# Reading LayerNorm rows back from DRAM as two transfers instead of one

## The chip, the cores and the metric

The kernel runs on one core of a Trainium2 chip. A core has a matrix engine (PE, with its weight loads shown as PEld), a vector engine (DVE), an activation engine (ACT), a general engine (POOL) and a queue engine (SP) that issues most of the DMA transfers; each works through its own list of instructions in order and waits on counters that the others raise. The metric is the device time of one execution in microseconds (us). A profile shows one execution; times inside it are counted from the start of its span.

## The reference

Two layers of sliding-window attention and two of a dense MLP follow each other, with the same weights both times. Input is one sequence of 2048 tokens of 512 channels in bf16; there are 32 heads of 16 channels, a window of 256 tokens and 1792 hidden channels.

```python
def _A_ref(x, wqkv, wo):
    H = 32; Dh = D // H; W = 256
    qkv = (x @ wqkv).reshape(B, S, 3, H, Dh).transpose(2, 0, 3, 1, 4)
    q, k, v = qkv[0], qkv[1], qkv[2]
    scores = jnp.einsum("bhqd,bhkd->bhqk", q, k) * (Dh ** -0.5)
    mask = (idx[:, None] - idx[None, :] >= 0) & (idx[:, None] - idx[None, :] < W)
    p = _softmax(jnp.where(mask[None, None], scores, -1e9), axis=-1)
    return jnp.einsum("bhqk,bhkd->bhqd", p, v).transpose(0, 2, 1, 3).reshape(B, S, D) @ wo

def _B_ref(x, w1, b1, w2, b2):
    return _gelu(x @ w1 + b1) @ w2 + b2

x = x + _A_ref(_layernorm(x), A_wqkv, A_wo)
x = x + _B_ref(_layernorm(x), B_w1, B_b1, B_w2, B_b2)
x = x + _A_ref(_layernorm(x), A_wqkv, A_wo)
x = x + _B_ref(_layernorm(x), B_w1, B_b1, B_w2, B_b2)
```

## The kernel before

The tokens are cut into 16 tiles of 128 rows. Counted over the two rounds there are 32 tiles (`tau`), and each passes two LayerNorms: one ahead of the attention (layer 0) and one ahead of the MLP (layer 1). The residual stream `X` and all weights stay in on-chip memory (SBUF).

Attention works in blocks of two tiles. For a block, PE makes queries, keys and values from the normalised, transposed rows `xnTA`; it then makes scores in visits of 512 columns (`ps<-QT,KT` in the profile), ACT takes their exponentials (line 946, `E<-ps`), DVE or POOL multiply the mask (line 967), PE multiplies by the values (`ps<-E,Va`), DVE transposes and normalises the result, and PE projects it with `Wo`. The MLP runs in jobs of two or four tiles: PE multiplies the rows `xnTB` by `W1` (shown as `ps<-xnTB,W_sb`), ACT applies the gelu (lines 1104 and 1112), PE multiplies by `W2` (`ps<-W_sb,gT`), and DVE adds the residual (line 788). The work of MLP jobs is laid in between the visits of later attention blocks, so that PE has something to do while ACT takes exponentials.

The matrix products need the normalised rows with channels on the partitions, that is transposed. `layernorm` (from line 726) makes mean and variance on DVE (lines 732 and 734), the reciprocal root on POOL (line 739) and the scaled rows `xn` on DVE (line 742). Then there are two ways. For the first tiles and the last two, PE transposes through PSUM. For the others (`by_dma`), DVE transposes blocks of 32 x 32 into `xs_` (line 751), SP writes `xs_` to one of eight scratch buffers in DRAM (line 756), and SP reads the scratch back into `xnTA` or `xnTB` in another layout (line 758). The write has 128 rows of 1 KB. The read fills, on each of the 128 partitions, four row groups (`r` in the code) of 256 bytes; in DRAM the four groups lie one after the other, so each group is a contiguous quarter of the scratch buffer. The 44 tiles that take this way give 44 writes and 44 reads, 26 into `xnTB` and 18 into `xnTA`.

The order in which the work is issued is written out by hand: `ORDER` lists all 3239 operations, `TURNS` picks the engine where there is a choice, and `BANKS` gives the PSUM banks. `_List.run` walks that list and computes a planned start and end of each operation from its planned duration `dur` and, for a transfer, the time `issue` after which SP is taken to be free; the plan does not change the order. `_Sched.op` then turns dependences into waits. Each transfer gets one of 16 counters in turn, and raises it by 16 once it has landed; whoever needs the data waits for the counter's value. `spread` may move a PE wait to an earlier matmul if the plan says that it will be over by then.

Both transfers of a tile go through SP's queue in order, with the other tiles' transfers and the output's (lines 1127 and 1141). A read first waits on SP until its write has landed, and while SP waits, everything listed behind it waits too.

Of the kernel before, what the change touches and what calls it, by code (L numbers as in the profile page):

```python
# [55 lines left out]
class _Sched:  # L56
# [29 lines left out]
                    kn[c2] = v2  # L86
        return True

    def op(self, eng, fn, reads=(), writes=(), inc=1, dma=False, start=0.0, end=0.0, n=1, joins=(), behind=None):
        kn = self.know[eng]  # L90
        req = {}

        def need(c, v):
            if v > 0 and kn.get(c, 0) < v and req.get(c, 0) < v:
                req[c] = v

        counter = eng
        if dma:
            counter = "dma%d" % (self.dma_rr % self.N_DMA_SEMS)
            self.dma_rr += 1  # L100
            inc = 16
            need(counter, self.cnt_val[counter])
        held = [self.res_w[r] for r in reads if r in self.res_w]
        for w in writes:
            if w in self.res_w:
                held.append(self.res_w[w])
            held += self.res_r.get(w, {}).items()
        for c, v in held:
            if not c == eng == "pe":
                need(c, v)  # L110
        for r in joins:
            need(*self.res_w[r])
        if behind is not None:
            need(*behind)
        waits = sorted(req.items(), key=lambda x: -self.when[x])
        waits = [(c, v) for c, v in waits if self._acquire(eng, c, v)]
        val = self.cnt_val[counter] + inc
        self.cnt_val[counter] = val
        self.snap[(counter, val)] = dict(kn)
        self.when[(counter, val)] = end  # L120
        for r in reads:
            d = self.res_r.setdefault(r, {})
            if d.get(counter, 0) < val:
                d[counter] = val
        for wr in writes:
            self.res_w[wr] = (counter, val)
            self.res_r[wr] = {}
        self.prog[eng].append(dict(fn=fn, waits=waits, counter=counter, inc=inc, start=start, n=n))
        return counter, val

    def wait_all_dma(self, eng):
# [32 lines left out]
    def emit(self):  # L164
        nc = self.nc
        self.spread()
        with nc.Block() as block:
            for eng in self.ENGINES:
                prog = self.prog[eng]

                def run(e, _prog=prog, _pe=eng == "pe"):
                    for o in _prog:
                        if _pe:
                            r = o["fn"](_Slots(e, o["at"]))
                        else:
                            for c, v in o["waits"]:
                                e.wait_ge(self.cnt_sem[c], v)
                            if o["fn"] is None:
                                continue
                            r = o["fn"](e)  # L180
                        r.then_inc(self.cnt_sem[o["counter"]], o["inc"])

                block._start_engine(run, _ENG_TYPES[eng])


class _List:
# [11 lines left out]
        self.lr = {}  # L198

    def add(self, eng, fn, dur, reads=(), writes=(), prio=0.0, alloc=(), free=(), after=(), geo=None, table=None,  # L200
            issue=0.0, alt=(), war=(), lock=False, joins=()):

        i = len(self.nodes)
        deps = set(after)
        for r in tuple(reads) + tuple(joins):
            if r in self.lw:
                deps.add(self.lw[r])
        for w in tuple(writes) + tuple(war):
            if w in self.lw:
                deps.add(self.lw[w])  # L210
            deps.update(self.lr.get(w, ()))
        for r in reads:
            self.lr.setdefault(r, []).append(i)
        for w in writes:
            self.lw[w] = i
            self.lr[w] = []
        deps.discard(i)
        n = 0
        if eng == "pe":
            c = _Count()  # L220
            fn(c, _Anywhere())
            n = c.n
        self.nodes.append(dict(
            eng=eng, fn=fn, dur=dur, reads=list(reads), writes=list(writes), prio=prio, joins=tuple(joins),
            jdeps=frozenset(self.lw[r] for r in joins), alloc=alloc, free=tuple(free), deps=deps, geo=geo, table=table,
            issue=issue, lock=lock, alts=((eng, fn, dur),) + tuple(alt), n=n, behind=None,
            heavy=any(a[0] == "pool" and a[2] > 600.0 for a in ((eng, fn, dur),) + tuple(alt)),
        ))
        return i
# [69 lines left out]
def bass_interleave_layers__sliding_block__dense_activation_gelu__prompt_kernel(  # L299
# [13 lines left out]
    P = 128  # L313
# [61 lines left out]
    with ExitStack() as kctx:  # L375
# [255 lines left out]
        add = PL.add  # L631
# [45 lines left out]
        for n, took in ((8, 3560.0), (3, 1280.0)):  # L677
            add("pe", clear(n), took, reads=["zero", "g0"], writes=["ps:init0", "ps:init1"], prio=-200, geo="f")

        def dma(fn, writes, reads=(), dur=2200.0, prio=0.0, issue=640.0, eng="sp"):  # L680
            add(eng, fn, dur, reads=reads, writes=writes, prio=prio, issue=issue)

        queued = {"sp": 0, "act": 0}

# [40 lines left out]
        def layernorm(tau, layer, dst, dname, prio):  # L725

            t = tau % T
            k = 2 * tau + layer
            s = xn_rr[0] % NXN
            xn_rr[0] += 1  # L730
            k6 = xn_rr[0] % 8
            add("dve", lambda e, B: e.bn_stats(stat6[:, k6, :], X[:, t, :]), 590,  # L732
                reads=["X%d" % t], writes=["st%d" % k6], prio=prio)
            add("dve", lambda e, B: e.bn_aggr(statmv[:, k, :], stat6[:, k6, :]), 95,
                reads=["st%d" % k6], writes=["mv%d" % k], prio=prio - 300)
            eps = lambda e, B: e.tensor_scalar(  # L736
                out=statmv[:, k, 1:2], in0=statmv[:, k, 1:2], scalar1=EPS, scalar2=None, op0=ALU.add)
            add("dve", eps, 75, reads=["mv%d" % k], writes=["ve%d" % k], prio=prio - 300, alt=(("pool", eps, 130),))
            add("pool", lambda e, B: e.tensor_tensor(  # L739
                out=statmv[:, k, 1:2], in0=statmv[:, k, 1:2], in1=mhalf[:], op=ALU.pow), 535,  # L740
                reads=["ve%d" % k, "mhalf"], writes=["rs%d" % k], prio=prio - 500)
            scale = lambda e, B: e.tensor_scalar(
                out=xn[:, s, :], in0=X[:, t, :], scalar1=statmv[:, k, 0:1], scalar2=statmv[:, k, 1:2],
                op0=ALU.subtract, op1=ALU.mult)
            add("dve", scale, 325, reads=["X%d" % t, "mv%d" % k, "rs%d" % k], writes=["xn%d" % s], prio=prio, lock=True)
            g = "tp%d" % k
            if by_dma(tau, layer):
                z = xs_rr[0] % NXS
                v = xs_rr[0] % NSC
                xs_rr[0] += 1  # L750
                add("dve", lambda e, B: e.transpose(  # L751
                    xs_[:, z, :].rearrange("p (q d j) -> p d q j", q=4, d=DC), xn[:, s, :].rearrange("p (d j q) -> p d q j", q=4, d=DC)), 630,
                    reads=["xn%d" % s], writes=["xs%d" % z], prio=prio)
                flat = scr[v].rearrange("p c -> (p c)")
                room = 0.0 if tau < 12 else 700.0
                dma(lambda e, B: e.dma_start(scr[v], xs_[:, z, :]),
                    ["scr%d_0" % v], reads=["xs%d" % z], prio=prio, dur=2200.0 + room, issue=400.0)
                dma(lambda e, B: e.dma_start(dst.rearrange("p r d j -> p r (d j)"), flat.rearrange("(r p c) -> p r c", r=4, p=P)),
                    [dname], reads=["scr%d_0" % v], prio=prio, dur=2700.0 + 2 * room, issue=400.0)
                return  # L760
            def tr(e, B):
                for c in range(DC):
                    r = e.transpose(psb[:, B[g][0], c * P : (c + 1) * P], xn[:, s, c * P : (c + 1) * P], ident[:])
                return r

            add("pe", tr, 4 * 56.0, reads=["xn%d" % s, "ident"], writes=["ps:" + g], prio=prio,
                alloc=[(g, 1)], geo="f", war=[dname])
            evac(lambda B: dst.rearrange("p r c j -> p c r j"),
                 lambda B: psb[:, B[g][0], 0 : DC * P].rearrange("p (c r j) -> p c r j", c=DC, r=4), 512,
                 ["ps:" + g], [dname], prio, free=[g], two=True, kind="t", boot=True)  # L770
# [386 lines left out]
        B = PL.gmap  # L1157
# [13 lines left out]
        for i in order:  # L1171
            nd = PL.nodes[i]
            n = 1
            if nd["eng"] == "pe":
# [1 line left out]
                nd["fn"](c, B)  # L1176
                n = c.n
            marks[i] = S_.op(nd["eng"], lambda e, fn=nd["fn"]: fn(e, B), reads=phys(nd["reads"]), writes=phys(nd["writes"]), dma=nd["issue"] > 0,
                  start=nd["start"], end=nd["vis"], n=n, joins=nd["joins"], behind=marks[nd["behind"]])
        S_.wait_all_dma("sp")  # L1180
        S_.emit()

# [27 lines left out]
```

## Time and profile before

| | us |
|---|---|
| median of 3 runs | 448.62 (447.82 to 449.89) |
| profiled execution | 448.7 |
| its span in the profile | 446.6 |
| PE busy in the span | 432.3 |
| ACT busy | 388.2 |
| DVE busy | 376.2 |
| POOL busy | 250.2 |

In the profile's rows, `L758` is line 758 of the kernel, an engine's name with a `q` at its end (`SPq`) is its sequencer issuing something, and `xnTB<-scr_x` is an operation that writes `xnTB` from `scr_x`. In rows of a timeline stand the start, the length, the engine, the line, the operation, the number of merged instructions (`x3`) and, in brackets, the idle time before it with what ended that. A row with three numbers and slashes gives the shortest, the median and the longest, in nanoseconds for durations. "DMA to landing" is the time from the start of the issue until the data has landed. A span's share of busy time does not say what is critical; the chain of work that ended last does, since it is followed back from the last instruction through whatever released each step.

### The profile page before, as it was taken

The page shows a single profiled execution, that of the slowest core. Times are in us where ns is not written, and L with a number is a line of the kernel's source. Part 1 is how long each engine was busy: PE and PEld are TensorE (multiplying, and loading weights), DVE is VectorE, ACT ScalarE, POOL GpSimd, SP SyncE. Part 2 cuts the span into 40 slices and gives each one's busy share as a digit, 9 for nine tenths or more (in the row PEclk, how much of TensorE's full clock was granted, in tenths as well). Part 3 has the DMA queues.
Part 4 walks back from the last instruction along what each step waited for, and adds up shares of the span by engine and source line. Part 5 has one row for each costly group of instructions (what it writes and reads, how often), then busy time and mean ns, then how long its engine had stood idle before and what let it go on. Part 6 is the DMA issues. An engine that isn't in the chain of part 4 may idle for free.

```text
span 446.6 us, 19315 instructions
## 1 busy us (share of the span) xinstructions
PE 432.3 (97%) x8762; PEld 230.7 (52%) x8762; DVE 376.2 (84%) x744; ACT 388.2 (87%) x457; POOL 250.2 (56%) x311
## 2 busy tenths in 40 slices
PE   7989999988999999999999999999999999999997
PEld 4545645645544555454445445445454454445664
DVE  6999989999997999889998999999898886687602
ACT  3999999999999989898998999889988998892442
POOL 5665875756888355363845682643448655562510
PEclk9999999999999999999999999999999999999999
DMA  9920000001120132001320002300222003102012
GB/s 260 370 94 4 4 1 4 4 15 26 46 66 13 27 86 63 25 10 32 95 51 3 26 25 65 83 4 13 73 62 62 15 3 84 28 3 86 13 35 70
DMA packets 39902, 22.87 MB, mean 51 GB/s; under 512 B 24588, under 2 KB 39308, under 8 KB 39820
## 3 DMA queue, kind: packets, MB, share of 16 engines
q1 hardware_dynamic: 39404, 21.24, 16.5%
q8 instruction: 68, 1.11, 1.0%
q10 hardware_dynamic: 416, 0.39, 0.3%
q14 instruction: 14, 0.11, 0.1%
HBM read 13.77 MB, written 7.86 MB: 48 GB/s over the span
## 4 chain that ended last, share of the span: by engine, by line
PE 70%; ACT 21%; DVE 4%; DMA 3%; issue 1%; POOL 1%
PE ps L32 70%; ACT E L946 13%; ACT gT L1104 3%; ACT gT L1112 2%; ACT L946 1%; DMA scr_x<-xs_ 1%; DMA xnTB<-scr_x 1%; ACT L1104 1%; DVE stat L732 1%; DMA X<-in_A_x_dram 1%; PE ps L36 1%; DVE TT L1032 1%; DVE E L967 0%; DVE X L788 0%; DVE xs_ L751 0%
## 5 line engine op out<-in xcount | busy, mean ns | idle before, releaser
L946 ACT ACTIVATE E<-ps 128x1024 bf16<-128x1024 f32 x304 | 286.2, 1054 | 19.8 <-PE ps L32 18.8
L967 POOL TENSOR_TENSOR E<-E,mask 128x512 bf16<-128x512 bf16 (+1 forms) x142 | 147.2, 1055 | 81.5 <-DVE E L967 31.4
L32 PE MATMUL ps<-W_sb,gT 128*128 128x512 bf16 (+2 forms) x462 | 118.9, 374 | 0.5 <-ACT E L946 0.5
L32 PE MATMUL ps<-xnTB,W_sb 128*128 128x512 bf16 (+1 forms) x560 | 114.1, 337 | 1.1 <-DMA xnTB<-scr_x 1.0
L32 PEld LDWEIGHTS ps<-xnTB,W_sb 128*128 128x128 bf16 x560 | 51.3, 98 | 45.5 <-ACT E L946 3.3
L32 PE MATMUL ps<-xnTA,Wqkv_sb 128*128 128x256 bf16 (+1 forms) x544 | 73.3, 267 | 1.0 <-ACT E L946 0.7
L32 PE MATMUL ps<-QT,KT 32*64 32x320 bf16 (+4 forms) x2976 | 65.3, 258 | 2.7 <-ACT E L946 1.6
L788 DVE TENSOR_TENSOR X<-X,ps 128x512 bf16<-128x512 bf16 x63 | 42.4, 677 | 24.5 <-PE ps L32 23.2
L32 PEld LDWEIGHTS ps<-W_sb,gT 128*128 128x128 bf16 x462 | 40.2, 98 | 42.7 <-issue 6.4
L32 PEld LDWEIGHTS ps<-xnTA,Wqkv_sb 128*128 128x128 bf16 x544 | 46.8, 98 | 22.3 <-issue 3.7
L1112 ACT ACTIVATE gT<-ps,b1T 128x512 bf16<-128x512 f32 (+1 forms) x68 | 36.4, 584 | 23.5 <-PE ps L32 23.4
L1076 POOL TENSOR_TENSOR X<-X,b2b 128x512 bf16<-128x512 bf16 x32 | 36.7, 1155 | 31.7 <-DVE E L967 20.0
L32 PEld LDWEIGHTS ps<-QT,KT 32*64 32x64 bf16 x2976 | 27.8, 103 | 49.5 <-ACT E L946 33.4
L1101 DVE TENSOR_SCALAR gT<-ps,b1T 128x512 bf16<-128x512 f32 (+1 forms) x72 | 45.2, 650 | 9.0 <-PE ps L32 8.3
L967 DVE TENSOR_TENSOR E<-E,mask 128x512 bf16<-128x512 bf16 (+1 forms) x120 | 46.2, 412 | 3.9 <-ACT E L946 3.7
L1032 DVE STREAM_TRANSPOSE TT<-ps 128x1024 f32<-128x1024 f32 x32 | 39.8, 1245 | 10.0 <-PE ps L32 9.7
L32 PE MATMUL ps<-E,Va 64*17 64x128 bf16 (+3 forms) x3872 | 46.1, 229 | 2.3 <-ACT E L946 1.2
L32 PEld LDWEIGHTS ps<-E,Va 64*17 64x17 bf16 x3872 | 36.8, 85 | 18.9 <-PE ps L32 7.3
L732 DVE BATCH_NORM_STATS2 stat<-X 128x6 f32<-128x512 bf16 x64 | 43.1, 681 | 2.3 <-DMA X<-in_A_x_dram 2.0
L739 POOL TENSOR_TENSOR statmv<-statmv,mhalf 128x1 f32<-128x1 f32 x64 | 37.1, 586 | 10.9 <-DVE statmv L736 7.6
L862 DVE TENSOR_TENSOR KT<-ps,parmask 128x1024 bf16<-128x1024 f32 x30 | 36.2, 1207 | 1.5 <-PE ps L32 0.9
L32 PE MATMUL ps<-Wo_sb,OT 128*128 128x512 bf16 x128 | 36.3, 380 | 0.2 <-ACT E L946 0.2
(55 smaller groups left out, 343.4 us busy)
## 6 DMA issues: line engine op xcount, KB each, us to landing
scr_x<-xs_ SPq DMA_DIRECT2D x44, 128.0 KB, 2.0
W_sb<-in_B_w_dram SPq DMA_DIRECT2D x2, 1792.0 KB, 15.6
xnTB<-scr_x SPq DMA_DIRECT2D x26, 128.0 KB, 2.7
xnTA<-scr_x SPq DMA_DIRECT2D x18, 128.0 KB, 2.6
out_dram<-X SPq DMA_DIRECT2D x15, 128.0 KB, 1.8
Wqkv_sb<-in_A_wqkv_dram SPq DMA_DIRECT2D x4, 256.0 KB, 4.9
X<-in_A_x_dram SPq DMA_DIRECT2D x1, 1024.0 KB, 9.1
Wqkv_sb<-in_A_wqkv_dram SPq DMA_DIRECT2D x1, 512.0 KB, 6.4
```

The lines of the kernel that those rows point to most:

```text
L32: return self.e.matmul(*a, **k)
L732: add("dve", lambda e, B: e.bn_stats(stat6[:, k6, :], X[:, t, :]), 590, reads=["X%d" % t], writes=["st%d" % k6], prio=prio)
L739: add("pool", lambda e, B: e.tensor_tensor(out=statmv[:, k, 1:2], in0=statmv[:, k, 1:2], in1=mhalf[:], op=ALU.pow), 535, reads=["ve%d" % k ...
L788: add("dve", lambda e, B: e.tensor_tensor(out=X[:, t, :], in0=X[:, t, :], in1=ps[:, B[g][0], :], op=ALU.add), d_psum(512), reads=["X%d" % ...
L862: add("dve", lambda e, B, g=g, i=i: e.tensor_tensor(out=KT[:, kb, :, 2 * i : 2 * i + 2, :].rearrange("p a c q -> p a (c q)"), in0=ps[:, B[ ...
L946: add("act", lambda e, B, g_=g_, gi=gi: e.activation(E[:, 2 * gi : 2 * gi + 2, e0 : e0 + 512], ps[:, B[g_][0] : B[g_][0] + 2, :], AF.Exp, ...
L967: op = lambda e, B, Ew=Ew, Mw=Mw: e.tensor_tensor(out=Ew, in0=Ew, in1=Mw, op=ALU.mult)
L1032: add("dve", lambda e, B: e.transpose(TT[:, s].rearrange("p a c q d -> p a (c q d)"), ps[:, B[g][0] : B[g][0] + 2, :].rearrange("p a n -> ...
L1076: add("pool", lambda e, B: e.tensor_tensor(out=X[:, t, :], in0=X[:, t, :], in1=b2b[:], op=ALU.add), 1110, reads=["X%d" % t, "b2b"], writes ...
L1101: add("dve", lambda e, B, g=g, fc=fc: e.tensor_scalar(out=gT[:, fc, 0:M], in0=ps[:, B[g][0], 0:M], scalar1=b1T[:, fc : fc + 1], scalar2=No ...
L1104: add("act", lambda e, B, fcs=fcs: e.activation(gT[:, fcs[0] : fcs[-1] + 1, 0:M], gT[:, fcs[0] : fcs[-1] + 1, 0:M], AF.Gelu_apprx_tanh, sc ...
L1112: add("act", lambda e, B, g=g, fc=fc: e.activation(gT[:, fc, 0:M], ps[:, B[g][0], 0:M], AF.Gelu_apprx_tanh, bias=b1T[:, fc : fc + 1], scal ...
```

## The change

Each read is issued as two transfers, one for row groups 0 and 1, one for groups 2 and 3, right behind each other on SP. Both raise the same counter, by 16 each, so the read now counts 32 and whoever waits for it waits for both. The planned issue time of a read goes from 400 to 760 ns; the order list, the engine choices and the banks stay as they are. `_Sched.op`, `_List.add` and the emission learn a number of `parts`. In the changed file the write stands in line 757 and the reads in line 761.

```diff
         if dma:
             counter = "dma%d" % (self.dma_rr % self.N_DMA_SEMS)
             self.dma_rr += 1
-            inc = 16
+            inc = 16 * parts
             need(counter, self.cnt_val[counter])
...
-                        r.then_inc(self.cnt_sem[o["counter"]], o["inc"])
+                        for x in r if isinstance(r, list) else [r]:
+                            x.then_inc(self.cnt_sem[o["counter"]], o["inc"] // o["parts"])
...
-        def dma(fn, writes, reads=(), dur=2200.0, prio=0.0, issue=640.0, eng="sp"):
-            add(eng, fn, dur, reads=reads, writes=writes, prio=prio, issue=issue)
+        def dma(fn, writes, reads=(), dur=2200.0, prio=0.0, issue=640.0, eng="sp", parts=1):
+            add(eng, fn, dur, reads=reads, writes=writes, prio=prio, issue=issue, parts=parts)
...
                 dma(lambda e, B: e.dma_start(scr[v], xs_[:, z, :]),
                     ["scr%d_0" % v], reads=["xs%d" % z], prio=prio, dur=2200.0 + room, issue=400.0)
-                dma(lambda e, B: e.dma_start(dst.rearrange("p r d j -> p r (d j)"), flat.rearrange("(r p c) -> p r c", r=4, p=P)),
-                    [dname], reads=["scr%d_0" % v], prio=prio, dur=2700.0 + 2 * room, issue=400.0)
+                def read(e, B):
+                    to, frm = dst.rearrange("p r d j -> p r (d j)"), flat.rearrange("(r p c) -> p r c", r=4, p=P)
+                    return [e.dma_start(to[:, i : i + 2, :], frm[:, i : i + 2, :]) for i in (0, 2)]
+
+                dma(read, [dname], reads=["scr%d_0" % v], prio=prio, dur=2700.0 + 2 * room, issue=760.0, parts=2)
                 return
```

More of the change, by code (lines that the diff above doesn't have):

```diff
@@ L87, in _acquire, with op @@
         return True
-    def op(self, eng, fn, reads=(), writes=(), inc=1, dma=False, start=0.0, end=0.0, n=1, joins=(), behind=None):
+    def op(self, eng, fn, reads=(), writes=(), inc=1, dma=False, start=0.0, end=0.0, n=1, joins=(), behind=None, parts=1):
         kn = self.know[eng]
@@ L127, in op @@
             self.res_r[wr] = {}
-        self.prog[eng].append(dict(fn=fn, waits=waits, counter=counter, inc=inc, start=start, n=n))
+        self.prog[eng].append(dict(fn=fn, waits=waits, counter=counter, inc=inc, start=start, n=n, parts=parts))
         return counter, val
@@ L200, in add @@
     def add(self, eng, fn, dur, reads=(), writes=(), prio=0.0, alloc=(), free=(), after=(), geo=None, table=None,
-            issue=0.0, alt=(), war=(), lock=False, joins=()):
+            issue=0.0, alt=(), war=(), lock=False, joins=(), parts=1):
         i = len(self.nodes)
@@ L225, in add @@
             jdeps=frozenset(self.lw[r] for r in joins), alloc=alloc, free=tuple(free), deps=deps, geo=geo, table=table,
-            issue=issue, lock=lock, alts=((eng, fn, dur),) + tuple(alt), n=n, behind=None,
+            issue=issue, lock=lock, alts=((eng, fn, dur),) + tuple(alt), n=n, behind=None, parts=parts,
             heavy=any(a[0] == "pool" and a[2] > 600.0 for a in ((eng, fn, dur),) + tuple(alt)),
@@ L1178, in bass_interleave_layers__sliding_block__dense_activation_gelu__prompt_kernel @@
             marks[i] = S_.op(nd["eng"], lambda e, fn=nd["fn"]: fn(e, B), reads=phys(nd["reads"]), writes=phys(nd["writes"]), dma=nd["issue"] > 0,
-                  start=nd["start"], end=nd["vis"], n=n, joins=nd["joins"], behind=marks[nd["behind"]])
+                  start=nd["start"], end=nd["vis"], n=n, joins=nd["joins"], behind=marks[nd["behind"]], parts=nd["parts"])
         S_.wait_all_dma("sp")
```

## The prediction

> **What bounds the kernel now.** I read the page first, then who waited for whom, then the chain of work that ended last in order of time, then the SP queue's timeline around the places where that chain runs through a transfer, and last what the PE does after each read has landed.
>
> ```profile
> span 446.6 us, 19315 instructions
> PE 432.3 (97%) x8762; PEld 230.7 (52%) x8762; DVE 376.2 (84%) x744; ACT 388.2 (87%) x457; POOL 250.2 (56%) x311
> PE 70%; ACT 21%; DVE 4%; DMA 3%; issue 1%; POOL 1%
> scr_x<-xs_ SPq DMA_DIRECT2D x44, 128.0 KB, 2.0
> xnTB<-scr_x SPq DMA_DIRECT2D x26, 128.0 KB, 2.7
> xnTA<-scr_x SPq DMA_DIRECT2D x18, 128.0 KB, 2.6
> ```
>
> The PE is busy 97% of the span, with ACT near behind, and DMA is 3% of the chain. The changed reads are the last two rows: 26 + 18 = 44 reads of 128 KB, each behind one of the 44 writes.
>
> ```profile
> PEld ps L32 <- ACT E L946: 49.3, 138, 0.8
> PEld ps L32 <- DMA xnTB<-scr_x: 1.4, 2, 1.1
> PE ps L32 <- DMA xnTB<-scr_x: 1.0, 1, 1.0
> ```
>
> Columns: total us, times, longest. TensorE waits for these reads only twice, 0.3 and 1.1 us by its weight loads. That caps what any earlier landing can save at 1.4 us. The chain shows where:
>
> ```profile
> 118.92 2.83 DMA scr_x<-xs_
> ...
> 121.77 2.66 DMA xnTB<-scr_x
> ...
> 124.47 3.14 PE ps L32 x88
> ...
> 127.66 24.09 PE ps L32 x426
> ...
> 175.67 2.96 DMA scr_x<-xs_
> ...
> 178.65 2.27 DMA xnTB<-scr_x
> ...
> 180.97 4.51 PE ps L32 x64
> ...
> 309.13 112.50 PE ps L32 x2158
> ```
>
> Columns: start, length, what. I call 117 to 124 place one and 171 to 181 place two. At both, a write and then a read stand on the chain, and PE work follows at once; after each the chain stays on PE and ACT to the end. So a microsecond lost here is taken as a microsecond at the end, one for one.
>
> **The change part by part.** *Forty-four more issues on SP.* Each read becomes two transfers of 64 KB. SP issues in order, so what an issue occupies is charged to whatever stands behind it.
>
> ```profile
> 119.29 1.67 SPq L758 DMA_DIRECT2D xnTB<-scr_x  x1
> 121.00 0.51 SPq L758 DMA_DIRECT2D xnTB<-scr_x  x1
> 121.77 0.36 SPq L758 DMA_DIRECT2D xnTB<-scr_x  x1
> 174.71 0.37 SPq L758 DMA_DIRECT2D xnTB<-scr_x  x1
> 175.18 0.45 SPq L758 DMA_DIRECT2D xnTA<-scr_x  x1
> 175.67 0.50 SPq L756 DMA_DIRECT2D scr_x<-xs_  x1
> 277.70 2.16 SPq L758 DMA_DIRECT2D xnTB<-scr_x  x4
> 315.85 0.37 SPq L758 DMA_DIRECT2D xnTA<-scr_x  x1
> 316.26 0.51 SPq L758 DMA_DIRECT2D xnTA<-scr_x  x1
> ```
>
> An issue on a quiet queue takes 0.36 to 0.37 us, one behind another about 0.5, and four reads in a row took 2.16, so 0.54 each. The issue of a write, with other row sizes, takes 0.50 behind a read as well, so I do not expect a half to issue in half the time: 0.54 for each added issue in a burst, with 0.27 (half the bytes, half the time) as the low end. Over the kernel that is 44 x 0.54 = 24 us of SP, nearly all beside SP's idle time; it counts only where a critical transfer stands behind.
>
> *Landing of a half.* No row has a 64 KB read. The nearest are a read alone (2.3 us after its start), a full read directly behind another (3.0), a write directly behind a read (2.2) and a write alone (1.7), in this order:
>
> ```profile
> DMA to landing us min/median/max: 2.3/2.3/2.3
> ...
> L758 SPq DMA_DIRECT2D xnTA<-scr_x x1: 508/508/508, 316.3 to 316.3; - x1
> ...
> DMA to landing us min/median/max: 3.0/3.0/3.0
> ...
> L756 SPq DMA_DIRECT2D scr_x<-xs_ x1: 504/504/504, 221.2 to 221.2; - x1
> ...
> DMA to landing us min/median/max: 2.2/2.2/2.2
> ...
> L756 SPq DMA_DIRECT2D scr_x<-xs_ x1: 332/332/332, 188.1 to 188.1; - x1
> ...
> DMA to landing us min/median/max: 1.7/1.7/1.7
> ```
>
> For the second half I take 2.2 us after its own start, as for the write behind a read; ends 1.7 and 2.7 (the third read of place one). The pair at 315.85 starts 0.41 apart, so a split read that stands alone lands 0.41 + 2.2 = 2.6 after its start where the whole one took 2.27: +0.3 (ends -0.2, from 0.41 + 1.7, and +0.6, halfway between a read alone, 2.3, and the whole pair, 0.41 + 3.0 = 3.4).
>
> *Place one.* Three reads become six issues. The first read's issue ends at 119.29 + 1.67 = 120.96; no row explains its length, and I leave it to the first half as it is. Its second half, the second read and the first half of the third are four more issues: 4 x 0.54 puts the start of the last half at 123.12, against 121.77 for the whole third read. The write that this read waits for has landed at 121.75 by the chain, so SP itself becomes what is late. Landing 123.12 + 2.2 = 125.3 against 121.77 + 2.66 = 124.43: +0.9. The PE has no room: its scores end at 123.99 + 0.43 = 124.42, and W1 starts at 124.47.
>
> ```profile
> 123.99 0.43 PE L32 MATMUL ps<-QT,KT 32*64 32x64 bf16 x24 [0.31 <-ACT E L946]
> ...
> 124.47 0.11 PEld L32 LDWEIGHTS ps<-xnTB,W_sb 128*128 128x128 bf16 x2 [0.29 <-DMA xnTB<-scr_x]
> ...
> 173.71 0.70 DVE L751 STREAM_TRANSPOSE xs_<-xn 128x512 bf16<-128x512 bf16 x1
> ...
> 180.97 1.47 PE L32 MATMUL ps<-xnTB,W_sb 128*128 128x512 bf16 x6 [0.98 <-DMA xnTB<-scr_x]
> ```
>
> Ends: 0 (halves issue in half the time, so the burst is as long as before) and +1.4 (landing keeps 2.7).
>
> *Place two.* The write at 175.67 is late already: its rows were ready at 173.71 + 0.70 = 174.41, and SP was busy with two reads. Two more issues move it by 2 x 0.54 = 1.1 to 176.75. It took 2.96 to land behind two whole reads; I take 2.2 again, since the halves ahead have had 1.1 us more to drain: 178.95 against 178.63, +0.3 (ends -0.2, from 176.75 + 1.7, and +1.1, with 2.96 kept). Then the critical read itself, +0.3 as above (ends -0.2 and +0.6). Together +0.6 (ends -0.4 and +1.7), on top of the 0.98 that the PE waits there now.
>
> *All other reads* land earlier than they are needed. The closest rows (each landing stands beside the start of the PE work that needs it):
>
> ```profile
> L758 SPq DMA_DIRECT2D xnTB<-scr_x x1: 360/360/360, 380.4 to 380.4; - x1
> ...
> DMA to landing us min/median/max: 3.0/3.0/3.0
> ...
> 384.79 1.46 PE L32 MATMUL ps<-xnTB,W_sb 128*128 128x512 bf16 x6
> ```
>
> 380.4 + 3.0 = 383.4 leaves 1.3 us. The write ahead of it also stands behind two reads, so the price is that of place two, +0.6, covered by the 1.3; at the upper end, 1.7, some 0.4 comes through.
>
> *Counters and waits.* A read now raises its counter by 32, and every wait for it asks for the second half too: no added wait. The instruction order of all engines is kept. The longer planned issue (760 for 400) moves four PE waits to a neighbouring matmul, one of them in place one, where the wait for the second read goes from the last score matmul to the first of W1. Cost 0, hidden as PE would stop at the next matmul anyway.
>
> **Sum.** 0.9 + 0.6 = +1.5 us on the profiled execution's 448.7 (span 446.6 and 2.1 around it), so 450.2; that execution stands 0.1 above the median of the runs, 448.62. Ends: -0.4 gives 448.3, and 1.4 + 1.7 + 0.4 = 3.5 gives 452.2.
>
> **The rivals.** *Issue is hidden* (chance 0.25): the halves issue fast enough and the engines carry the same bytes, so both places stay; 448.7, give or take 0.5. For it: outside the bursts SP has little to do (nothing between 176.17 and 178.65 in place two). Against: place two has a write that waits 1.3 us behind SP's own issues. [...]
>
> *Halves land sooner* (chance 0.08), the other side. If a second half lands less than 2.27 - 0.41 = 1.86 us after its start, the split read beats the whole one. With the 1.7 of the write alone it gains 0.2 at place two in the read and 0.2 in the write: 448.3. All waits gone would be 448.7 - 1.4 = 447.3. Against: a half does not stand alone, it follows its sister on the queue.
>
> *Bursts collide* (chance 0.20): landings keep their long values behind other traffic (2.7 at place one, 2.96 for the write at place two) and the room of 1.3 at 380.4 is used up. That is the upper sum, 452.2, decided by whether the write at place two lands nearer to 2.2 or to 3.0 after its start.
>
> **How the numbers follow.** The forecast of 450.2 gets 0.47, with its own range 449.3 to 451.2. With the rivals the range is 448.3 to 452.2. Half a per cent is 2.2 us, about what a measurement of this kernel can tell from no change. Slower by more than that means above 450.9: the collisions, 0.20, and about 0.07 of the forecast's upper edge, 0.27. Faster by more than that would be under 446.4, beyond the 447.3 that the reads' waits allow; 0.04 for shifts I cannot see. The rest, 0.69, is within it.
>
> **What would show it.** In the changed profile: 88 read issues of 64 KB, the second of each pair near 0.5 us; the burst at 119.29 some 1.4 us longer; W1 of place one starting near 125.3, with a PE wait of about 0.9 for the read; in place two the write starting 2.0 us after the read that is now at 174.71, where it starts 0.96 after it today, and a PE wait of about 1.6 in place of 0.98. The forecast is wrong if the issues in a burst take about 0.3 each, if second halves land under 1.9 us after their start, or if the PE waits for reads at a third place.

## The result and the profile after

The changed kernel takes 450.04 us (median; 449.40 to 456.00) where the kernel before takes 448.63 beside it: a ratio of 1.0040, with an interval of 1.0021 to 1.0060. That is 1.4 us slower, within the half per cent that the prediction called no change, and 0.2 below its 450.2. Two executions, 452.59 and 456.00, stand apart from the rest; their mean granted TensorE clock was 0.996 and 0.992 where the others have 0.999 or 1 (called full clock below), and what lies behind that is a part of the experiments.

The profiled execution took 449.73 with a span of 448.0 (before: 448.7 and 446.6). From the page of the changed kernel, its busy times, its chain by engine and its transfers:

```profile
span 448.0 us, 19286 instructions
PE 423.4 (95%) x8690; PEld 231.5 (52%) x8762; DVE 376.5 (84%) x744; ACT 388.3 (87%) x457; POOL 250.1 (56%) x311
PE 65%; ACT 17%; DVE 11%; issue 2%; DMA 2%; SPq 1%; POOL 1%
xnTB<-scr_x SPq DMA_DIRECT2D x52, 64.0 KB, 2.3
xnTA<-scr_x SPq DMA_DIRECT2D x36, 64.0 KB, 2.3
```

The 44 reads are now 52 + 36 = 88 transfers of 64 KB. DVE, ACT and POOL are busy as before; PE's lower figure goes with 72 matmul records that are missing (8690 against 8762), so it isn't compared. New on the chain is SP's own issuing (`SPq` 1%). Who waited for whom (total us, times, longest):

```profile
PEld ps L32 <- DMA xnTB<-scr_x: 2.2, 2, 1.3
```

TensorE still waits for the reads at two places only, now 2.2 us where it was 1.4 by the weight loads. The chain of work that ended last, at place one and place two (start, length, what):

```profile
119.44 1.61 SPq L761
121.10 0.47 SPq L761
...
122.64 0.47 SPq L761
123.15 2.08 DMA xnTB<-scr_x
125.27 3.13 PE ps L32 x87
...
177.00 2.45 DMA scr_x<-xs_
179.46 0.36 SPq L761
179.86 2.47 DMA xnTB<-scr_x
182.38 3.66 PE ps L32 x38
```

At place one, the write that stood there before is gone from the chain and five issues of SP have taken its place: SP itself is what is late. From the second on (121.10; three later 122.64; the last half 123.15) they start 0.51 apart, and the last half lands 2.08 after its start. From the burst's start to the landing it is 123.15 + 2.08 - 119.44 = 5.79; before it was 121.77 + 2.66 - 119.29 = 5.14. At place two the SP queue runs like this (start, length, merged issues), first the write of before that stands ahead of the read at 174.71, and then the changed kernel:

```profile
171.10 0.32 SPq L756 DMA_DIRECT2D scr_x<-xs_  x1
```

```profile
172.36 0.33 SPq L757 DMA_DIRECT2D scr_x<-xs_  x1
172.73 2.04 SPq L761 DMA_DIRECT2D xnTA<-scr_x  x2
175.05 0.88 SPq L761 DMA_DIRECT2D xnTB<-scr_x  x2
176.03 0.93 SPq L761 DMA_DIRECT2D xnTA<-scr_x  x2
177.00 0.47 SPq L757 DMA_DIRECT2D scr_x<-xs_  x1
179.46 1.33 SPq L761 DMA_DIRECT2D xnTB<-scr_x  x2
```

The write now starts 177.00 - 175.05 = 1.95 after the read ahead of it (0.96 before). The split read behind it, from its first half's start at 179.46 to the second half's landing at 179.86 + 2.47 = 182.33, takes 2.87, where the whole read took 2.27. Its second half's issue alone took 1.33 - 0.40 = 0.93 (the halves start 0.40 apart), and not the 0.47 of an issue behind another; the last section has what stood beside it.

Where the 1.4 us came in is seen by setting the same PE work of the two profiles side by side. From PE's timelines, before (beside the rows of 123.99, 124.47 and 180.97 above):

```profile
159.67 1.46 PE L32 MATMUL ps<-W_sb,gT 128*128 128x512 bf16 x6
161.06 0.53 PE L32 MATMUL ps<-QT,KT 32*64 32x256 bf16 x16
...
179.56 0.43 PE L32 MATMUL ps<-QT,KT 32*64 32x256 bf16 x24
```

and after:

```profile
124.15 0.43 PE L32 MATMUL ps<-QT,KT 32*64 32x64 bf16 x24 [0.31 <-ACT E L950]
125.27 1.47 PE L32 MATMUL ps<-xnTB,W_sb 128*128 128x512 bf16 x6 [0.70 <-DMA xnTB<-scr_x]
...
160.47 1.46 PE L32 MATMUL ps<-W_sb,gT 128*128 128x512 bf16 x6 [0.16 <-issue]
162.43 0.40 PE L32 MATMUL ps<-QT,KT 32*64 32x256 bf16 x10 [0.27 <-issue]
...
180.80 0.43 PE L32 MATMUL ps<-QT,KT 32*64 32x256 bf16 x24
182.38 1.47 PE L32 MATMUL ps<-xnTB,W_sb 128*128 128x512 bf16 x6 [1.15 <-DMA xnTB<-scr_x]
```

The lag is 0.16 ahead of place one, 125.27 - 124.47 = 0.80 behind it, still 0.80 at 160.47, 1.24 ahead of place two, 1.41 behind it, and 1.4 at the end (448.0 - 446.6). So place one brought 0.64, place two only 0.17, and 0.44 came between them, where PE stopped in the middle of a group of 16 scores, ahead of 162.43, for no wait that the profile shows; before, the 16 ran through. In this one execution place two came off lightly because its transfers began early beside PE: the read at 175.05 is 0.34 later than before (174.71), while PE is 1.24 later, since the write ahead of it landed 175.05 - 172.36 = 2.7 after its start and not 3.6 (174.71 - 171.10). (Beside both a packet of instructions was loaded, as told below: it ended at 173.40 before and at 173.89 after, 1.3 and 1.2 ahead of the landing.) The path from that read to the landing of the critical one grew from 178.65 + 2.27 - 174.71 = 6.21 to 182.33 - 175.05 = 7.28. One profile can't settle how this divides on the average; the experiments go some of the way.

### The profile page after: what moved, and what is told of

Read it like the earlier page. It is cut to its first block, busy times and chain, and to the rows that moved or that the text cites. A ratio compares the mean times of both kernels' runs of the same rounds, so it can differ in the third digit from the quotient of the medians.

```text
span 448.0 us, 19286 instructions
## 1 busy us (share of the span) xinstructions
PE 423.4 (95%) x8690; PEld 231.5 (52%) x8762; DVE 376.5 (84%) x744; ACT 388.3 (87%) x457; POOL 250.1 (56%) x311
## 4 chain that ended last, share of the span: by engine, by line
PE 65%; ACT 17%; DVE 11%; issue 2%; DMA 2%; SPq 1%; POOL 1%
PE ps L32 64%; ACT E L950 9%; ACT gT L1108 3%; DVE TT L1036 2%; ACT gT L1116 2%; ACT L950 1%; DVE OT L1046 1%; DVE E L971 1%; DVE KT L866 1%; DMA xnTB<-scr_x 1%; DVE xs_ L752 1%; DVE stat L733 1%; ACT L1108 1%; SPq L761 1%; DVE X L792 1%
## 5 line engine op out<-in xcount | busy, mean ns | idle before, releaser
L32 PE MATMUL ps<-W_sb,gT 128*128 128x512 bf16 (+2 forms) x422 | 109.1, 373 | 5.3 <-issue 4.1
L1041 POOL TENSOR_TENSOR TM<-TT,Rc 128x512 bf16<-128x512 f32 x19 | 20.1, 1057 | 28.6 <-DVE Rc L1039 10.9
```

Of the source, the lines that this page charges most:

```text
L32: return self.e.matmul(*a, **k)
L1041: mul = lambda e, B: e.tensor_tensor(out=TM[:, sm].rearrange("p c q a d -> p a (c q) d"), in0=TT[:, s, :, :, :, 0:Dh].rearrange("p a c q d ...
```

## The experiments

My theory was that the 1.4 us is two prices, SP's longer burst at place one and the moved write with the longer critical read at place two. Against it stood: the plan's longer issue time moves PE's waits and that costs; the added issues cost everywhere, a little each; one of the two places holds it all.

**The plan alone.** The halves stay, and the planned issue goes back to 400, so that all PE waits stand where they stood before.

```diff
-                dma(read, [dname], reads=["scr%d_0" % v], prio=prio, dur=2700.0 + 2 * room, issue=760.0, parts=2)
+                dma(read, [dname], reads=["scr%d_0" % v], prio=prio, dur=2700.0 + 2 * room, issue=400.0, parts=2)
```

> All reads split, but the planned issue time of a read stays at 400 ns as before the change, so that every wait stays on the instruction where it stood before. Queue theory (the cost is SP's added issues ahead of the transfers that place one and place two wait for): 450.0 us, as the changed kernel, W1 of place one some 0.6 to 0.8 us later than before. Plan theory (the cost is the four PE waits that the longer planned time moves): back to 448.6.

Measured: 450.31, ratio 1.0036 (1.0019 to 1.0053) to 448.94 of before on that chip. The cost is all there without the moved waits; they cost nothing that can be told.

**Which reads.** The next three kernels split only some reads, by tile and layer, and leave the others whole. The edit is the same but for the set:

```diff
+                two = (tau, layer) in ((4, 1), (6, 1), (7, 1))
                 def read(e, B):
                     to, frm = dst.rearrange("p r d j -> p r (d j)"), flat.rearrange("(r p c) -> p r c", r=4, p=P)
+                    if not two:
+                        return e.dma_start(to, frm)
                     return [e.dma_start(to[:, i : i + 2, :], frm[:, i : i + 2, :]) for i in (0, 2)]
-                dma(read, [dname], reads=["scr%d_0" % v], prio=prio, dur=2700.0 + 2 * room, issue=760.0, parts=2)
+                dma(read, [dname], reads=["scr%d_0" % v], prio=prio, dur=2700.0 + 2 * room, issue=760.0 if two else 400.0, parts=2 if two else 1)
```

The set shown is place one's three reads. For place two it is `in ((10, 1), (11, 1), (18, 0), (19, 0))`, where (11, 1) is the critical read and the others are issued ahead of it; for the rest it is `not in` all these seven, which leaves 37 reads split.

> Only the three reads of the burst at place one are split, the other 41 stay whole. Queue theory: 0.7 us over the kernel before, 449.3, with the PE's wait for the read at place one near 0.9 us and place two as before, 1.0. Everywhere theory (each split read costs a little wherever it stands, 1.4 us over 44 reads): 3 of 44, so 0.1 us, 448.7.

> Only the four reads of place two are split (the three that follow one another from 171 to 176 and the one that W1 waits for at 179). Queue theory: 0.6 us by the forecast's sum, 449.2; by the changed kernel's trace, where the PE wait there grew from 0.98 to 1.2, only 0.2, 448.8. Everywhere theory: 4 of 44 of 1.4 us, 0.1.

> The 37 reads that are neither in place one nor in place two are split, those seven stay whole. Queue theory: nothing on the chain is behind an added issue, 448.6 give or take 0.2. Everywhere theory: 37 of 44 of 1.4 us, 449.8. If the 0.46 us for which the PE stops amid scores at 162 in the changed kernel comes from the split reads at 152 to 160, 449.1.

Measured against 448.94: place one 449.51, ratio 1.0015 (1.0002 to 1.0027); the rest 449.07, 1.0006 (0.9995 to 1.0017); place two 452.26, 1.0055 (1.0020 to 1.0089). In place one's profile the burst and the PE work behind it (SP's and PE's timelines):

```profile
119.23 4.26 SPq L764 DMA_DIRECT2D xnTB<-scr_x  x6
```

```profile
125.32 1.04 PE L32 MATMUL ps<-xnTB,W_sb 128*128 128x512 bf16 x4 [0.97 <-DMA xnTB<-scr_x]
```

Three split reads thus bring place one's delay whole, and 37 others bring nothing that stands clear of the noise. By a price everywhere, those 37 would have cost 37/44 x 1.4 = 1.2; their interval ends at 0.0017 x 448.94 = 0.8. So a price everywhere isn't the cause, though a small one isn't ruled out. Place two gave a surprise: its twelve executions fall into two groups, six at 448.5 to 450.3 with a granted clock of 0.999 or more, and six at 454.2 to 456.8 with 0.992 to 0.996. At full clock the median of the six is 449.5, +0.6. With 0.6 for place one and 0.1 for the rest the parts add up to 1.3, the same as the changed kernel's 449.9 at full clock (its 16 executions of that kind) less 448.6. So the sum of the two-price theory holds at full clock. Its second price is weakly founded, though: six executions, chosen by their clock, between 448.5 and 450.3, where the 35 of before lie between 448.0 and 450.0, so the +0.6 isn't told from zero. The low clock is something else; the kernel before never showed it (0.999 or more in its 35 executions).

**Twice the dose.** Four transfers of one row group each, for every read.

```diff
-                    return [e.dma_start(to[:, i : i + 2, :], frm[:, i : i + 2, :]) for i in (0, 2)]
+                    return [e.dma_start(to[:, i : i + 1, :], frm[:, i : i + 1, :]) for i in range(4)]
...
-                dma(read, [dname], reads=["scr%d_0" % v], prio=prio, dur=2700.0 + 2 * room, issue=760.0, parts=2)
+                dma(read, [dname], reads=["scr%d_0" % v], prio=prio, dur=2700.0 + 2 * room, issue=1480.0, parts=4)
```

> Every read issued as four transfers of one row group each. Queue theory: an added issue takes the 0.51 us that the changed kernel shows in a row. Place one: the last of twelve issues starts 1.66 + 10 x 0.51 = 6.8 us after the first and lands 2.1 later, 8.9 against 5.1 in the kernel before, +3.7. Place two: eight issues ahead of the write, +2.3, and three inside the last read, +1.2. The reads with 1.3 to 3 us of room lose it, 1 to 4 us more. In all 456 to 460 us. Everywhere theory (a fixed price for each added transfer, 1.4 us for 44, so 4.2 for 132): 453.

Measured: 477.99, ratio 1.0654 (1.0626 to 1.0683), far above what I expected. The SP queue, PE behind the burst, PE at place two, and who waited:

```profile
119.70 7.01 SPq L761 DMA_DIRECT2D xnTB<-scr_x  x12
```

```profile
128.50 2.41 PE L32 MATMUL ps<-xnTB,W_sb 128*128 128x512 bf16 x6 [3.67 <-DMA xnTB<-scr_x]
```

```profile
191.32 1.89 PE L32 MATMUL ps<-xnTB,W_sb 128*128 128x512 bf16 x4 [5.69 <-DMA xnTB<-scr_x]
```

```profile
PE ps L32 <- DMA xnTB<-scr_x: 19.9, 6, 5.7
```

The burst of twelve took 7.01 us, and place one's delay of 128.50 - 124.47 = 4.0 is close to the forecast of 3.7. But the room of the other reads is used up, so that PE now waits six times, and at four of these waits its work runs at half clock: behind place one's, six matmuls of W1 take 2.41 where they took 1.47. The windows' columns are length, busy time of PE, PEld, DVE, ACT and POOL with counts, granted clock, DMA share and GB/s:

```profile
191.30:197.00 5.70, 5.68 (x36) 1.93 (x37) 1.86 (x5) 2.29 (x3) 1.78 (x2) 0.50 0.00 0
```

While PE is busy all the time from 191.3 to 197.0 it is granted a clock of 0.50. By the trace's clock records, the stretches at half clock amid the work are 3.41, 6.83, 6.83 and 3.41 long, 20.5 in all, so 10.2 us are lost by them (the record has a mean clock of 0.978); the waits, 19.9 where there was 1.0 before, are the other 19, together the 29 that were lost (477.99 - 448.95). A second price thus stands behind these waits: the clock.

**Taking away what makes the write late.** In the order list of the kernel before, the write of place two is put ahead of the two reads that stand in front of it. The same three lines were then put into the changed kernel.

```diff
+        for x in (1156, 1321):
+            ORDER.remove(x)
+        ORDER[ORDER.index(1169) + 1 : ORDER.index(1169) + 1] = [1156, 1321]
```

> The kernel before, reads whole; in place two alone the order list puts the write of the last tile ahead of the two reads that stood before it on SP. If that write is late because of SP's queue, it starts at 174.4 instead of 175.7, the last read lands near 178.9, before the PE comes to W1 at 180.0, and the PE's wait of 0.98 us goes: 448.0 where the kernel before has 448.9. If the write's landing and not its issue sets the time: no change.

> All reads split, with the same reorder in place two. Queue theory: place two costs nothing and gives back the 0.98, place one keeps its 0.6: 448.9 + 0.1 + 0.6 - 1.0 = 448.6, so the changed kernel's whole loss is made up though all 88 reads stay. Everywhere theory: the loss of 1.4 stays and only the 0.98 goes, 449.3.

Measured: 448.56 with the kernel before, ratio 0.9993 (0.9980 to 1.0006); 450.39 with the changed one, 1.0028 (1.0011 to 1.0045), against 448.95. Neither gained what I expected. In the first the wait for the read has gone, but PE stopped one matmul later for something else:

```profile
PEld ps L32 <- DMA xnTB<-scr_x: 0.2, 1, 0.2
```

```profile
180.16 0.39 PE L32 MATMUL ps<-xnTB,W_sb 128*128 128x512 bf16 x1
181.10 1.25 PE L32 MATMUL ps<-xnTB,W_sb 128*128 128x512 bf16 x5 [0.55 <-issue]
```

So the wait of 0.98 at place two covered another stop, of 0.55, that the profile puts down to nothing. Such stops stand at the same instructions in several of the traces. Setting aside those of 0.42 and 0.32 that recur in nearly every profile, and those at half clock, the fourteen profiles have 25 of over 0.3, and each comes 1.2 to 1.7 us after a packet of 16 KB of instructions has been loaded. The stop at 162 is one of them: the packet ended at 160.92, and PE went on at 162.43. No run shows a link between the two. In the second kernel place two's wait fell to 0.52 in its profile, but the burst at place one took 4.43, 0.3 more than in the profile of the changed kernel, and the total did not come down; the table below shows where its profile lost it.

**The critical read alone, and the reads ahead of it.** Place two has two prices, the moved write and the split critical read. One kernel splits only `(11, 1)`, the other only `(10, 1), (18, 0), (19, 0)`.

> Only the one read that W1 waits for in place two is split; nothing stands behind it that is needed soon. The forecast's +0.3 us for a second half that starts 0.41 later and lands 2.2 after that: 449.2 where the kernel before has 448.9. By the second halves in the traces so far (2.2 to 2.6 after their start): +0.3 to +0.7.

> Only the three reads of place two that stand on SP ahead of the late write are split, the critical read stays whole. By the forecast the write starts 1.1 us later and lands 0.3 us later: +0.3, 449.2 where the kernel before has 448.9. If landing keeps its 2.96 us: +1.1, 450.0. If nothing but the split of the critical read counts in place two: no change.

Measured: the critical read alone 449.27, ratio 1.0006 (0.9992 to 1.0020) to 448.95, a +0.3 whose interval holds zero. The reads ahead alone 450.17, 1.0050 (1.0015 to 1.0084) to 448.55, again in two groups: six executions at full clock with a median of 448.95, +0.4, and five at 0.992 to 0.996 between 451.4 and 456.1. The low clock thus goes with the moved write, and not with the split of the critical read, as far as kernels that ran on different chips can tell that (chip 12 for the critical read, chip 5 for the reads ahead).

**Catching the low clock in a profile.** The kernel that splits all of place two was run twice more, the one that splits the reads ahead once more.

> A second look at the kernel with only place two's four reads split, of which half the executions took some 5 us more at a granted clock of 0.992 to 0.996. Place-two theory: in such an execution the PE's wait there is longer than 1.3 us and the half clock follows right behind it. Rival: the half clock sits elsewhere in the span, and the split reads are not its cause. If the look shows an execution at full clock: 449.5, wait 1.1 to 1.3.

> The same look once more, with the same two theories: a longer wait of the PE in place two with the half clock right behind it, or a half clock elsewhere in the span.

> A second look at the kernel with only the three reads ahead of the late write split, of which 5 of 11 executions ran at a granted clock of 0.992 to 0.996 and took 451 to 456 us. If the profile falls in such an execution, it shows where the half clock sits. Place-two theory: right behind the PE's wait near 181. Rival: elsewhere in the span. In an execution at full clock: 448.9, as the others there.

The first two came at full clock, 449.79 and 449.40, with waits of 0.97 and 1.12 at place two, and told nothing of the low one. The third caught it: 453.28, ratio 1.0094 (1.0058 to 1.0130) to 449.53, all three executions at 0.995 to 0.996. The chain and PE's timeline at place two of that profile:

```profile
176.88 4.14 DMA scr_x<-xs_
...
181.04 2.23 DMA xnTB<-scr_x
```

```profile
183.31 1.98 PE L32 MATMUL ps<-xnTB,W_sb 128*128 128x512 bf16 x6 [2.78 <-DMA xnTB<-scr_x]
185.80 3.17 PE L32 MATMUL ps<-xnTB,W_sb 128*128 128x512 bf16 x10
```

The same kernel at full clock had this row at the same place, and the ten matmuls of 185.80 took 2.33:

```profile
181.84 1.47 PE L32 MATMUL ps<-xnTB,W_sb 128*128 128x512 bf16 x6 [0.43 <-DMA xnTB<-scr_x]
```

The write took 4.14 to land, and so PE waited 2.78. Windows of the caught execution: the 3.41 us up to the change of the clock, the stretch at half clock, and the time behind it:

```profile
180.72:184.13 3.41, 0.82 (x4) 0.41 (x5) 1.08 (x2) 1.84 (x2) 0.00 (x0) 1.00 0.19 43
184.13:187.54 3.41, 3.41 (x32) 1.08 (x31) 1.78 (x5) 1.60 (x2) 1.19 (x2) 0.50 0.00 0
187.60:191.00 3.40, 3.40 (x43) 1.80 (x42) 2.19 (x6) 2.39 (x4) 1.21 (x2) 1.00 0.00 0
```

PE had 0.82 us of work in the first 3.41; 0.8 after it started again, the clock was 0.50 for 3.41 us and then 1.00. Half of 3.41 is 1.7 us lost, and the wait itself is 2.78 - 0.98 = 1.8 longer than before: 3.5 of the 451.0 - 446.6 = 4.4 by which this profile's span is longer than that of before. One stretch of 3.41 at half clock makes a mean of 1 - 1.7/451 = 0.996, and two would make 0.992; this estimate from one profile agrees with the two kinds of low clock in the executions, 0.995 to 0.996 and 0.992. That theirs sits at place two as well was seen in this one profile alone. What ran beside the write shows in the DMA view of 177.4 to 180.0, the busy tenths of the 16 engines in 40 slices and the queue that loads instructions:

```profile
DMA  3457985689999621100000000000000000000011
...
q8 instruction: 1, 0.02, 4.1%
```

The engines are all but empty in the second half of this stretch (one of 16 alone is less than a tenth), and yet the write does not land until 176.88 + 4.14 = 181.02. In the records of single packets, one of 16 KB of instructions started on one engine at 178.19, 1.3 after the write, and took 1.70; when it is over, at 179.89, data moves again (the last two slices), and the write lands 1.1 later. In other profiles that packet started later after this write: 1.5 in the profile with the shorter planned issue, 1.6 in the first two profiles of the kernel that splits place two, 2.0 in the changed kernel, 2.4 in the other profile of this same kernel; there the write landed 2.0 to 2.5 after its start. Before, it started 2.3 after the write, which landed at 178.63 while the packet still ran. So in the caught execution the write, started 1.2 later than before (176.88 for 175.67), stood 1.3 ahead of the packet's start and not 2.3. That late writes and packets go together is borne out by all the writes of the fourteen profiles, those of the kernel before too: of 590 whose landing is known, 265 had no such packet while they were under way, and none of them took more than 2.86; all 114 that took longer had one. (Some 210 had one and landed within 2.86 all the same.) Moving the packet was not tried, so that it held the write is read from the traces, not shown by an experiment.

**Where PE fell behind, profile by profile.** All fourteen traces have the same 8762 weight loads in the same order, so each can be set beside the same load in the profile of before. The table gives by how much PE's lag grew from ahead of each place to behind it, and at the end, in us; what is missing to the end arose elsewhere, up to 0.9 of it ahead of place one.

| reads split | place one | stop near 162 | place two | at the end |
|---|---|---|---|---|
| all (changed kernel) | 0.6 | 0.5 | 0.2 | 1.4 |
| all, shorter planned issue | 1.0 | 0.3 | -0.1 | 1.4 |
| all, write moved ahead | 1.4 | 0.6 | -0.5 | 2.2 |
| place one alone | 0.9 | 0.3 | -0.6 | 0.7 |
| the rest alone | 0.1 | 0.6 | 0.0 | 0.9 |
| place two alone (three profiles) | 0.1, 0.6, 0.0 | 0.1, 0.2, 0.0 | 0.1, 0.0, 0.1 | 1.2, 1.3, 1.1 |
| reads ahead alone, full clock | 0.4 | 0.1 | -0.6 | 0.7 |
| critical read alone | 0.1 | 0.1 | -0.1 | 0.5 |
| none, write moved ahead | 0.1 | 0.1 | -0.3 | -0.2 |

Where place one is split it costs 0.6 to 1.4, and elsewhere mostly 0.1, at most 0.6. Not all of it reaches the end: with place one alone split, PE came 1.2 late to place two and left it 0.5 late, since its wait there shrank from 0.98 to 0.37:

```profile
181.51 1.47 PE L32 MATMUL ps<-xnTB,W_sb 128*128 128x512 bf16 x6 [0.37 <-DMA xnTB<-scr_x]
```

At place two itself, split reads at full clock never cost more than 0.2. The 0.6 that the medians give for it is thus not borne out by the profiles, and what they show in its place is a wait that no longer shrinks when PE comes late (1.15 and 0.91 with all reads split). These are single executions, in which stops of 0.3 to 0.8 come and go, so how the 1.4 us divides beyond place one stays open.

## Why the prediction was right, and where it was not

*The total.* 450.2 forecast, 450.04 measured, and the case that was named likeliest is the one that came: SP late at place one, write and critical read later at place two. That the sum came within 0.2 owes something to luck: by the profiles, place two brought less than its +0.6, and the stop near 162, 0.3 to 0.6 where place one or the rest is split, had no term.

*Place one, +0.9.* The mechanism came step by step: five issues on the chain, the last half starting 123.15 - 119.44 = 3.71 after the burst's start where 3.83 was forecast, W1 at 125.27 where 125.3 was. The size was 0.64 in this profile; 0.12 of the difference is the issue in a row (4 x 0.03, as it is 0.51 and not 0.54) and 0.12 the landing of a half (2.08, not 2.2), both taken from whole reads and a write. The three other profiles with place one split have 0.9 to 1.4, so +0.9 was a fair size. What failed is "one for one": behind place one the chain runs through PE, DVE and POOL to the write of place two, where PE waits anyway, and with place one alone split 0.6 of the delay went into that wait.

*Place two, +0.6.* The write started 1.95 after the read (2.0 forecast). Its landing and the critical read were each put too low: 2.45 and 2.87 where I took 2.2 and 2.6, so that the path grew by 1.07 in the profile, of which 0.9 was taken up because it began earlier beside PE. The medians at full clock agree with the forecast, +0.6 with place two alone, 0.4 for the reads ahead and 0.3 for the critical read, but none of the three is told apart from zero, and the profiles have 0.2 at most. That the forecast met the medians here may be luck. The PE wait of 1.6 that I named did not show (1.15), for the same reason.

*All other reads, the waits, the counters: 0.* Right: +0.1 for 37 reads, not told apart from zero; no cost for the moved waits; no third place. No price came through the room of 1.3 us; with four transfers a read, PE waits at six places.

*Issue is hidden, halves land sooner.* Both fell. The issues did not shrink with the bytes (0.51 apart for 64 KB, 0.54 for 128 KB), and the split read took 2.87 for the 2.27 of the whole one. The DMA engines are busy for 16% of the span, and yet the split read lands 0.6 later, since its second half waits for its issue. The share is from the page of the changed kernel:

```profile
q1 hardware_dynamic: 40108, 21.25, 16.4%
```

*Bursts collide.* I gave this 0.20 as one way for the median to go. It is a thing of single executions: 2 of the 18 of the changed kernel, and 1 of 12 (453.83, clock 0.995) of the one with the shorter planned issue. Its place, the write of place two, was the one I named; its price was too low for such an execution: in the one that was caught, half clock (0.50 for 3.41 us) came with the wait of 2.78, and for that I had no term. Why the kernels that split place two alone are hit about every second time and the changed kernel rarely stays open. The distance of the instruction packet from the write doesn't sort them: it is 2.4 and 1.3 in two profiles of one kernel, and 1.5 in the one with the shorter planned issue. That place one's delay makes the difference was not tried.

## What to carry to other kernels

In this kernel, splitting a transfer on one queue did not halve its issue (0.51 us for 0.54 in a row): where several stood in a row and the last was on the chain, each piece added its half microsecond, and where one stood alone the second piece still started 0.4 later. Before an issue is added to a queue, look at what is queued behind it and how early each landing is beside the work that needs it; 37 of 44 reads had room and cost nothing that could be told, and what was shown by an experiment came from the three reads in a row. A delay isn't always handed on whole: a later place where the engine waits anyway can take it up. And PE bore waits of about 1 us at full clock, while one that grew by 1.8 to 2.8 us cost 3.5, so room is better judged against the latest landing than against the median one.

## What the runs showed of the hardware

**Issues in a row stood 0.51 us apart at 64 KB and 0.54 at 128 KB.** Reads of 128 KB start 0.54 apart in a burst (2.16 for four), those of 64 KB 0.51, and twelve of 32 KB with a long first one took 7.01 us; from the statistics of the issues of the changed kernel, where the median of 0.47 is that of an issue behind another:

```profile
L761 SPq DMA_DIRECT2D xnTB<-scr_x x52: 359/469/1695, 101.3 to 411.5; - x52
L761 SPq DMA_DIRECT2D xnTA<-scr_x x36: 359/469/1811, 125.6 to 340.0; - x36
...
DMA to landing us min/median/max: 1.8/2.3/3.8
```

**SP's long issues ended 0.2 to 0.4 us after a packet of instructions.** The longest issues, 1.70 and 1.81 in the rows above, and the 1.61 at 119.44 stand beside a median of 0.47 for the same reads. In the records of single packets, such a long issue ends about 0.4 us after an instruction packet of 16 KB does: before, the packet of 119.34 to 120.57 and the issue of 119.29 that ended at 120.96; after, the packets that ended at 120.68 and 173.89 and the issues that ended at 119.44 + 1.61 = 121.05 and at 174.26 (the first half of the pair at 172.73, which thus took 1.53). The second half of the critical read is another: 0.93, ending at 180.79, behind a packet that ended at 180.41. Over the fourteen profiles, 94 of the 1555 issues for these writes and reads took more than 0.8, and every one of them ended 0.2 to 0.4 after such a packet. This is a regularity of these traces; no run moved a packet.

**Half clock followed a wait of 2.51 us, and not one of 3.36.** In the caught execution the granted clock was 0.50 for 3.41 us after a wait of 2.78; it stayed at 1.00 after waits of 1.1 to 1.2. With four transfers a read, half clock followed a wait of 2.51 and not one of 3.36 (four matmuls in 1.04 us at full clock, six in 2.38 where full clock takes 1.47):

```profile
308.18 1.04 PE L32 MATMUL ps<-xnTB,W_sb 128*128 128x512 bf16 x4 [3.36 <-DMA xnTB<-scr_x]
411.77 2.38 PE L32 MATMUL ps<-xnTB,W_sb 128*128 128x512 bf16 x6 [2.51 <-DMA xnTB<-scr_x]
```

So the length of the wait alone does not sort the waits of these runs, and no run was made to find out what does. The stretches at half clock amid the work lasted 3.41 us in the caught execution, and 3.41 or 6.83 with four transfers a read.
